# Per-block tile counts, GpSimd's share and the planner's activity thresholds, changed together in a fused linear-attention and softmax-attention kernel

## Chip, core and metric

The kernel runs on one core of one Trainium2 chip. The metric is the device time of one execution in microseconds. Several executions are made, and their median is the time of the kernel.

## What is computed

There are two attention layers over the same input x (2048 rows, 512 columns, 32 heads of 16), mixed row by row by a gate:

```python
g = sigmoid((x * gate_w).sum(-1, keepdims=True))
# A: linear attention with softmax feature maps
phi_q = concat([softmax(q_A @ w_phi), softmax(-q_A @ w_phi)])   # phi_k alike
o_A = phi_q @ (phi_k.T @ v_A) / (phi_q @ phi_k.sum(0) + 1e-6)
# B: softmax attention, per head
p = softmax(q_B @ k_B.T * 16 ** -0.5)
o_B = p @ v_B
out = g * (o_A @ wo_A) + (1 - g) * (o_B @ wo_B)
```

Layer B needs 32 x 2048 x 2048 exponentials, and these set the work of ScalarE.

## The kernel before

**Tiling of B.** The heads come in four rows of eight. A block is one chunk of 512 queries with four heads, so that there are 32 blocks (NB). A block has 64 tiles: four heads times sixteen groups of 128 keys, each a 128 x 512 piece of the transposed scores. A score matmul (line 782) contracts only 16 of 32 rows, so up to four heads run beside each other in row strips of the array. The product with v (pv_mm, line 895) writes 32 rows of the one PSUM bank psO for each head, and four heads run beside each other in column strips. psO collects the whole block. When the block is complete, VectorE copies psO to Tf (line 979, add_norm), and only then can the next block start in psO.

**Two ways to an exponential.** Most tiles go to ScalarE. They are dealt in slots of alternately three and two tiles (line 727). A slot is one score op qk (add_qk), one ACTIVATE over the 3 or 2 PSUM banks (add_exp, line 874) and, for up to three slots together, one pv op (add_pv). The remaining tiles go to VectorE. DN, line 30, says how many of each block. They are taken in groups of four, the last of a block possibly of two (line 708). In a group, each tile has its own first step from PSUM to 16-bit integers (D1, line 840), and the group shares a mask (D2, line 855), a second mask (D3, line 857) and a product (D4). The product runs on VectorE (line 860), or, for the first PN[b] full groups of a block, as four quarters on GpSimd (line 863). Each VectorE tile gives two matmuls into psO (add_pvd, "term" ops); the block's last pv op waits for all of them.

**Buffers of the groups.** A group takes one buffer of each of three rings (line 747). Before block 13 (G_EARLY) the first two rings hold four buffers each, later four and three. make_groups(n) opens groups up to number n, and stops at the first whose buffers are still held. When a block opens in psO, groups are asked for up to the block's last number plus G_DEEP (line 968).

**Beside it.** Projections of B, the whole of layer A (phi, kv_half, q_rest), and the output projection (out_tile, out_part, out_last) are given to the same planner as fill ops, with due times counted in slots.

**The planner.** Plan.layout simulates the five engines with given durations and writes down an order for each engine; emit turns the orders into instruction streams with semaphore waits. On PE it chooses by priority: qk first, then what else is ready, and nothing that would make the next qk late (QK_TOL). It keeps a figure for the activity of PE over the last 3.41 us of its own time (WINDOW), as a weighted share:

```python
active = sum(w * (y - max(x, t - WINDOW)) for x, y, w in streams) / WINDOW
```

ACTIVE holds four thresholds for it. If PE has nothing to do and active is below ACTIVE[0], a round of four matmuls on the zero tile (line 885) is put in, into psO while a block is open there, otherwise into a free miscellaneous bank. Ahead of a pv op of an open block, more such rounds can stand:

```python
if op.room and t > 20.0 and active < ACTIVE[1]:
    op.extra = min(op.room, 1 if active > ACTIVE[2] else 2)
```

Riding means that an op shares a pass of the array with the one before it, in strips that this leaves free. The planner then counts only 0.02 us for it. Terms have exactly the priority T_PRIO, so that for them the last condition decides:

```python
if o.kind == want and not used_heads & set(o.heads) and o.ready <= pe_start + RIDE_TOL and (
        o.kind == "dq" or o.prio < T_PRIO or active >= ACTIVE[3]):
```

A first step's priority is its block's first slot minus D_AHEAD = 22 slots (d_prio), so VectorE works about one block ahead of ScalarE.

Of the kernel before, what the change touches and what calls it, by code (L numbers as in the profile page):

```python
# [26 lines left out]
EXPB = 127.0 * 2.0 ** 7 - 75.0  # L27
ESCALE = math.log(2.0) / 2.0 ** 7

DN = (0, 10, 14, 16, 14, 16, 14, 16, 14, 16, 14, 16, 14, 16, 14, 16, 14, 16, 14, 16, 14, 16, 14, 16, 14, 16, 14, 16, 14, 16, 14, 12)  # L30
G_EARLY = 13
W_AT = 18.0
D_FIRST = 12
# [1 line left out]
WINDOW = 3.41  # L35
ROWS = (0.0, 0.42, 0.65, 1.0, 1.15)
COLS = (0.0, 0.9, 1.25, 1.55, 1.55)
ACTIVE = (1.0, 0.64, 0.62, 0.54)
PE_CLASS = {"qk": 0, "dq": 0, "pv": 1, "term": 1, "zero": 1}
T_PRIO = 40.0  # L40
WARM = 4
# [8 lines left out]
DMA_PAD, T2_PAD = 1.0, 1.5  # L50
QK_TOL = (0.2, 0.65)
TURN_PAD = 4.0
G_DEEP = 6
K_AT, K_PACE, Q_AT, Q_PACE = 45.0, 13.0, 275.0, 13.5
PN = (1, 2, 1, 2, 1, 2, 1, 2, 1, 2, 1, 2, 1, 2, 1, 2, 1, 2, 1, 2, 1, 2, 1, 2, 1, 2, 1, 2, 1, 2, 1, 2)
D_AHEAD = 22.0
CONT = -60.0
EPAIRS = 5
# [44 lines left out]
class Plan:  # L103
# [44 lines left out]
    def layout(self):  # L148
# [19 lines left out]
        while left:  # L168
# [30 lines left out]
            for e in ENGINES:  # L199
# [11 lines left out]
                if e == "pe" and last_pe is not None and busy[e] > t - 1e-6:  # L211
                    want = {"qk": "dq", "dq": "dq"}.get(last_pe, "term")
                    for item in sorted(queues[e]):
                        o = item[2]
                        if o.kind == want and not used_heads & set(o.heads) and o.ready <= pe_start + RIDE_TOL and (
                                o.kind == "dq" or o.prio < T_PRIO or active >= ACTIVE[3]):
                            if o.acq is not None:
# [36 lines left out]
                busy_qk = e == "pe" and t < qk_at and t + 0.32 > qk_at + QK_TOL[qk_slot]  # L254
                if pick is None and e == "pe" and not busy_qk and zero_ok and t > 20.0 and active < ACTIVE[0]:
                    pick = Op("pe", 0.215, 1e9, self.idle, "idle")
# [4 lines left out]
                    left += 1  # L261
                if pick is None and e == "pe" and not busy_qk and not zero_ok and t > 20.0 and active < ACTIVE[0]:
                    bs = [b for b in self.misc if b.free and b.shared and all(o.end + LAT <= t for o in b.last)]
# [23 lines left out]
                if e == "pe":  # L287
                    if op.room and t > 20.0 and active < ACTIVE[1]:
                        op.extra = min(op.room, 1 if active > ACTIVE[2] else 2)
                        op.full += 0.215 * op.extra  # L290
# [110 lines left out]
def _build(ctx, nc, A_x, A_wqkv, A_w_phi, A_wo, B_wqkv, B_wo, gate_w, out):  # L401
# [295 lines left out]
    slots = []  # L697
    assert all(n % 2 == 0 for n in DN)
    dcount = [[0] * 4 for _ in range(NB)]
    dtiles, groups, turn = [], [], 0  # L700
    for b in range(NB):
        for k in range(DN[b]):
            i = (k + turn) % 4
            dcount[b][i] += 1
            dtiles.append(dict(t=(b, i, NT - dcount[b][i]), k=k))
        turn += DN[b]
        mine = dtiles[len(dtiles) - DN[b]:]
        for n in range(0, DN[b], 4):
            groups.append(dict(ts=mine[n:n + 4], left=len(mine[n:n + 4]), pool=n // 4 < PN[b] and len(mine[n:n + 4]) == 4))
    cur, rot = 0, 0  # L710
# [104 lines left out]
    def make_groups(n):  # L815
        for g in groups[made[0]:n]:
            if any(k in holder and holder[k]["left"] for k in (g["t"], g["s"])):
                break
            holder[g["t"]] = holder[g["s"]] = g
            add_group(g)  # L820
            made[0] += 1

    def d_prio(d):
        b = d["t"][0]
        return first_slot[b] + d["k"] * 20.0 / DN[b] - D_AHEAD

# [88 lines left out]
    def add_pv(js):  # L915
# [4 lines left out]
        for b, jmts in parts.items():  # L920
# [38 lines left out]
            if b not in full_start and all((b, i) in pv_started for i in range(4)):  # L959
# [7 lines left out]
                if mine:  # L967
                    make_groups(mine[-1]["g"]["n"] + G_DEEP)
            if js[0] == 0:
# [388 lines left out]
```

## Time and profile before

| what | us |
|---|---|
| median of 5 runs | 782.19 |
| lowest, highest | 780.57, 783.93 |
| the profiled execution | 781.67 |
| its span, first to last instruction | 779.8 |
| ACT busy | 758.3 |
| PE busy | 753.6 |
| DVE busy | 676.0 |
| POOL busy | 352.2 |
| mean granted TensorE clock, share of full | 0.991 |

The span is shorter than the profiled execution's time, because the time also holds what lies around the instructions. Busy times are of one engine each and overlap. ACT is ScalarE, PE is TensorE (PEld its weight loads), DVE is VectorE and POOL is GpSimd. A busy PE includes the zero matmuls. The profile also gives the clock that TensorE was granted in each stretch, as a share of full speed.

### The profile page before, as it was taken

Reading aid. Unit: us, or ns where it says so; the run is one execution under the profiler, and the core shown is the slowest. Engines: PE = TensorE matmul, PEld = TensorE weight load, DVE = VectorE, ACT = ScalarE, POOL = GpSimd, SP = SyncE. Lnnn points to the kernel's source line nnn. Section 1 sums busy time; section 2 is a strip of 40 time slices with the busy share of each in tenths; the row PEclk is TensorE's granted clock in tenths of the full one; section 3 lists DMA queues with packets and bytes.
Section 4 is the critical chain, followed back from the end, with each engine's and each line's share of the span. In section 5 each row is a group of like instructions: output and inputs, shape, how many; then the busy total and the mean of one; then the engine's idle time right before and its main releaser. Section 6 shows DMA issues by size and latency. Waiting matters only on the chain.

```text
span 779.8 us, 17665 instructions
## 1 busy us (share of the span) xinstructions
PE 753.6 (97%) x7342; PEld 232.5 (30%) x7342; DVE 676.0 (87%) x1098; ACT 758.3 (97%) x708; POOL 352.2 (45%) x329
## 2 busy tenths in 40 slices
PE   8999999999999999999999999999999999999999
PEld 4332223323332222333222232223223223222223
DVE  3678898899989999799999897999999899899793
ACT  5999999999999999999999998999999999999995
POOL 6133634536354564443734626455364443124332
PEclk9999999999999999999999998999999999999999
DMA  6600001000000000200001312231322231020001
GB/s 128 145 9 16 20 11 24 9 19 12 9 17 10 23 8 9 71 8 23 23 24 47 74 54 45 61 58 60 71 69 61 52 77 36 29 57 16 24 21 48
DMA packets 67935, 30.74 MB, mean 39 GB/s; under 512 B 53208, under 2 KB 62808, under 8 KB 67856
## 3 DMA queue, kind: packets, MB, share of 16 engines
q1 hardware_dynamic: 66368, 28.95, 15.6%
q8 instruction: 57, 0.93, 0.5%
q10 hardware_dynamic: 1104, 0.66, 0.3%
q14 instruction: 22, 0.18, 0.1%
q0 software_dynamic: 384, 0.02, 0.1%
HBM read 7.87 MB, written 8.88 MB: 21 GB/s over the span
## 4 chain that ended last, share of the span: by engine, by line
ACT 76%; PE 19%; DVE 3%; issue 1%; DMA 0%; SPq 0%; DVEq 0%
ACT E_t L874 72%; PE psS L782 6%; PE psO L895 6%; ACT EA_t L1117 4%; PE psO L885 3%; PE psS L590 2%; PE psM L590 2%; DVE Tx_t L840 1%; PE psM L782 1%; DMA phiK_t<-in_A_x_dram 0%; DVE oA_t L1205 0%; PE psS L1231 0%; DVE Ty_t L857 0%; DVE vA_t L855 0%; PE psM L885 0%
## 5 line engine op out<-in xcount | busy, mean ns | idle before, releaser
L874 ACT ACTIVATE E_t<-psS 128x1536 bf16<-128x1536 f32 x637 | 729.7, 1340 | 6.8 <-PE psS L782 5.3
L782 PE MATMUL psS<-qz_t,kTB_t 32*128 32x512 bf16 x1816 | 286.7, 386 | 19.3 <-ACT E_t L874 15.8
L863 POOL TENSOR_TENSOR Tx_t<-Tx_t,vA_t 128x512 bf16<-128x512 bf16 x116 | 132.9, 1167 | 125.2 <-DVE Ty_t L857 48.4
L885 PE MATMUL psO<-xT_t,zero_t 128*32 128x512 bf16 x1720 | 150.8, 385 | 0.0
L782 PEld LDWEIGHTS psS<-qz_t,kTB_t 32*128 32x128 bf16 x1816 | 71.5, 91 | 250.3 <-ACT E_t L874 196.6
L895 PE MATMUL psO<-E_t,vaug_t 128*32 128x512 bf16 (+1 forms) x1592 | 140.8, 389 | 0.2 <-DVE vaug_t L646 0.2
L840 DVE TENSOR_SCALAR Tx_t<-psM 128x512 int16<-128x512 f32 x129 | 87.7, 679 | 12.2 <-PE psM L782 9.3
L840 DVE TENSOR_SCALAR Tx_t<-psS 128x512 int16<-128x512 f32 x119 | 81.2, 682 | 11.0 <-PE psS L782 9.3
L782 PE MATMUL psM<-qz_t,kTB_t 32*128 32x512 bf16 x232 | 89.5, 386 | 1.0 <-DVE qz_t L687 0.5
L863 POOL TENSOR_TENSOR oT_t<-oT_t,WoB_t 128x512 bf16<-128x512 bf16 x44 | 51.2, 1181 | 51.8 <-DVE oT_t L857 27.5
L1122 POOL TENSOR_TENSOR half_t<-EA_t 128x512 f32<-128x512 bf16 x32 | 37.0, 1156 | 61.3 <-ACT EA_t L1117 32.1
L885 PEld LDWEIGHTS psO<-xT_t,zero_t 128*32 128x32 bf16 x1720 | 38.6, 94 | 63.9 <-issue 53.4
L1130 POOL TENSOR_TENSOR phiK_t<-EA_t,stat_t 128x512 bf16<-128x512 bf16 x32 | 34.9, 1090 | 44.3 <-DVE WoB_t L855 13.5
L895 PE MATMUL psO<-Tx_t,vaug_t 128*32 128x512 bf16 x248 | 53.2, 394 | 0.0
L995 POOL TENSOR_TENSOR oT_t<-Tf_t,Rb_t 128x512 bf16<-128x512 f32 x15 | 19.1, 1272 | 68.9 <-DVE vA_t L860 48.0
L895 PEld LDWEIGHTS psO<-E_t,vaug_t 128*32 128x32 bf16 (+1 forms) x1592 | 29.3, 95 | 58.1 <-issue 53.0
L863 POOL TENSOR_TENSOR Tx_t<-Tx_t,WoB_t 128x512 bf16<-128x512 bf16 x28 | 31.8, 1155 | 31.7 <-DVE Ty_t L857 20.8
L1130 POOL TENSOR_TENSOR phiQ_t<-EA_t,stat_t 128x512 bf16<-128x512 bf16 x32 | 33.9, 1058 | 26.5 <-DVE stat_t L1126 8.6
L857 DVE TENSOR_SCALAR Ty_t<-Tx_t 128x2048 int16<-128x2048 int16 x50 | 39.3, 796 | 0.1
L895 PE MATMUL psO<-Ty_t,vaug_t 128*32 128x512 bf16 (+1 forms) x284 | 38.8, 386 | 0.0
L782 PEld LDWEIGHTS psM<-qz_t,kTB_t 32*128 32x128 bf16 x232 | 21.1, 91 | 33.8 <-issue 12.9
L840 DVE TENSOR_SCALAR WAT_t<-psM 128x512 int16<-128x512 f32 x39 | 26.7, 684 | 4.8 <-PE psM L782 4.3
(184 smaller groups left out, 910.1 us busy)
## 6 DMA issues: line engine op xcount, KB each, us to landing
dpq<-phiQ_t SPq DMA_DIRECT2D x16, 256.0 KB, 2.2
Rb_t<-lr SPq DMA_DIRECT2D x120, 32.0 KB, 1.8
dpo<-oA_t SPq DMA_DIRECT2D x16, 128.0 KB, 1.8
qz_t<-qz_t SPq DMA_DIRECT2D x120, 16.0 KB, 1.8
Tf_t<-Tf_t SPq DMA_DIRECT2D x60, 32.0 KB, 2.0
out_dram<-WvA_t SPq DMA_DIRECT2D x14, 128.0 KB, 1.7
WB_t<-in_B_wqkv_dram SPq DMA_DIRECT2D x3, 384.0 KB, 4.9
WvA_t<-in_A_wqkv_dram SPq DMA_DIRECT2D x1, 512.0 KB, 4.0
```

Of the source, the lines that this page charges most:

```text
L590: return [lambda e, ap, i=i: e.matmul(ap, lhsT=lhs[i], rhs=rhs[i], start=(i == 0), stop=(i == len(lhs) - 1)) for i in range(len(lhs))]
L782: return e.matmul(bank, lhsT=kT_B[32 * i:32 * i + 32, b // 8 % 2, 128 * kt:128 * (kt + 1)], rhs=qz[32 * i:32 * i + 32, b // 2 % 4, b % 2, ...
L840: ops.append(drain(f, mm, "dve", 0.70, d_prio(d), lambda e, ap, q=q: e.tensor_scalar(quarter(tb, q).bitcast(I16), ap, EXPB, 0.0, op0=ALU.a ...
L857: add(0.72 if full else 0.45, lambda e: e.tensor_single_scalar(shaped(si16, si16), shaped(ti16, si16), 0x7F80, ALU.bitwise_and), tk, [g["s ...
L863: ops.append(P.add("pool", 1.1, d_prio(g["ts"][0]) - 5.0, lambda e, q=q: e.tensor_tensor(quarter(t4, q), quarter(t4, q), quarter(m4, q), A ...
L874: op = P.add("act", 0.051 + 0.4267 * n, 0.0, lambda e: e.activation(Ebuf[:, j // 2 % EPAIRS, 1536 * (j % 2):1536 * (j % 2) + 512 * n], psS ...
L885: ins = e.matmul((psO if bank is None else bank)[32 * i:32 * i + 32, :], lhsT=zero[:], rhs=xT[:, 0, 0:NQ], start=bank is not None, stop=ba ...
L895: return e.matmul(psO[32 * i:32 * i + w, :], lhsT=vaug[:, kt, o:o + w], rhs=rhs, start=start, stop=stop, tile_position=(0, 32 * i), skip_g ...
L995: P.add("pool", 1.1, -40, lambda e: e.tensor_tensor(oT[:, r, qc, :], Tf[:, 0, :], Rb[:], ALU.mult), reads=[("Tf", 0), "Rb"], writes=[("oT" ...
L1117: ins = e.activation(EA[:, b, :].rearrange("p (g s c) -> p s g c", s=2, c=64)[:, sgn, :, :], ap.rearrange("p (g c) -> p g c", c=64), ACTF. ...
L1122: P.add("pool", 1.15, prio, lambda e: e.tensor_tensor(half[:], e3[:, :, 0:8], e3[:, :, 8:16], ALU.add), reads=[("EA", b)], writes=["half"] ...
L1130: parts.append(P.add("pool", 1.0, prio, lambda e, n=n: e.tensor_tensor(dst[:, 512 * n:512 * n + 512].rearrange("p (g f) -> p g f", f=DH), ...
```

## The change

Only five constants of the planner are changed. DN sets how many tiles of each of the 32 blocks are taken by VectorE. PN sets how many of a block's full groups have their product on GpSimd. ACTIVE holds the thresholds described above. G_DEEP says how many groups beyond a block are asked for ahead.

```diff
-DN = (0, 10, 14, 16, 14, 16, 14, 16, 14, 16, 14, 16, 14, 16, 14, 16, 14, 16, 14, 16, 14, 16, 14, 16, 14, 16, 14, 16, 14, 16, 14, 12)
+DN = (0, 10, 12, 16, 10, 16, 12, 16, 14, 16, 14, 16, 14, 16, 14, 16, 14, 16, 14, 18, 14, 16, 14, 16, 14, 18, 12, 18, 14, 16, 18, 14)
...
-ACTIVE = (1.0, 0.64, 0.62, 0.54)
+ACTIVE = (1.0, 0.66, 0.72, 0.2)
...
-G_DEEP = 6
+G_DEEP = 5
...
-PN = (1, 2, 1, 2, 1, 2, 1, 2, 1, 2, 1, 2, 1, 2, 1, 2, 1, 2, 1, 2, 1, 2, 1, 2, 1, 2, 1, 2, 1, 2, 1, 2)
+PN = (2, 2, 1, 2, 1, 2, 1, 2, 1, 2, 1, 2, 1, 2, 1, 2, 1, 2, 1, 2, 0, 2, 1, 2, 1, 2, 1, 2, 2, 2, 1, 0)
```

In DN the entries of blocks 2, 4, 6, 19, 25, 26, 27, 30 and 31 differ; in PN those of blocks 0, 20, 28 and 31. No instruction is written differently; the planner lays out all streams anew from these values.

## Prediction

> **What bounds the kernel now.** I read first the page's busy times, then ScalarE's waits, then ScalarE and the clock by stages, then the chain that ended last, then the groups by form. The page's first part:
>
> ```profile
> span 779.8 us, 17665 instructions
> PE 753.6 (97%) x7342; PEld 232.5 (30%) x7342; DVE 676.0 (87%) x1098; ACT 758.3 (97%) x708; POOL 352.2 (45%) x329
> ```
>
> ACT and PE both show 97%, but PE's share contains filler: the group of matmuls on the zero tile (line 885) alone is 150.8 us busy. The waits of ScalarE:
>
> ```profile
> ACT E_t L874 <- PE psS L782: 5.3, 5, 2.0
> ACT WvA_t L1065 <- PE psS L590: 5.1, 1, 5.1
> ACT xT_t L1220 <- PE psS L1214: 2.5, 2, 1.3
> ...
> ACT qz_t L669 <- PE psM L662: 2.0, 1, 2.0
> ACT E_t L874 <- PE psM L782: 0.8, 1, 0.8
> ACT E_t L874 <- PE psO L895: 0.2, 1, 0.2
> ```
>
> Columns: total us, times, longest. Of the 5.3 us, 2.0 stand ahead of the very first exp (timeline: it starts at 11.73 us). All that ScalarE loses to PE between the first and the last exp is therefore 5.3 - 2.0 + 0.8 + 0.2 = 4.3 us. Where? The stages of 20 us (busy us and counts of PE, PEld, DVE, ACT, POOL; then the granted TensorE clock) are full for ACT except here:
>
> ```profile
> 440.00:460.00 20.00, 19.12 (x190) 5.55 (x189) 17.26 (x37) 19.47 (x18) 11.24 (x11) 0.91 0.20 52
> 460.00:480.00 20.00, 18.98 (x170) 5.18 (x169) 16.44 (x36) 17.65 (x17) 8.99 (x8) 0.83 0.14 43
> ...
> 720.00:740.00 20.00, 19.08 (x170) 5.29 (x169) 14.45 (x23) 18.87 (x18) 8.04 (x8) 0.91 0.09 23
> ```
>
> ACT lacks 0.53, 2.35 and 1.13 us, 4.0 of the 4.3, in just the three stages whose clock is below 1. Cut finer, the second is
>
> ```profile
> 469.51:472.92 3.41, 3.04 (x10) 0.67 (x10) 2.14 (x5) 3.31 (x4) 3.41 (x4) 0.66 0.03 5
> 472.92:476.33 3.41, 3.41 (x23) 0.59 (x22) 1.76 (x3) 1.95 (x2) 1.35 (x2) 0.50 0.05 12
> ```
>
> The clock is at half, and ACT works 1.95 of 3.41 us. The mean clock of 0.991 gives (1 - 0.991) x 779.8 / 0.5 = 14 us at half clock in all, about four stretches of 3.4 us. Each of the three places follows the copy of psO to Tf (line 979) that ends a block: 444.85, 468.99 and 727.83 us in the timeline. The copies run from 42.2 (block 0) to 727.8 (block 29), 23.6 us apart, so these are the ends of blocks 17, 18 and 29. While psO is being copied and has no open block, the planner has no bank for its zero matmuls, and PE stood empty for about 0.7 us at 445.4 and 468.9, 0.6 at 728.3.
>
> The remaining span is head (11.73 us), ScalarE's own work, and a tail of 779.8 - 770.7 = 9.1 us from the last exp's end.
>
> **What the Trainium skill says.** "TensorE: Matmul & The Clock Gate", Part 1, says that an activity monitor gives the array half its pulses after an idle window and that the window is 3.41 us and free-running. The trace agrees on the size: the clock is 0.50 over such a stretch and is full again after one or two. It also means that where a dip falls in the window matters, so the count of half-clock stretches can differ between executions; the five times (780.57 to 783.93) spread by about the price of two or three. "ScalarE: Activation LUTs", the section on what ACT_TABLE_LOAD costs, gives 0.833 ns an element[...]; the forms below differ by 1550 - 1131 = 419 ns for one tile more. "Advanced Engine Details and Errata", VectorE Performance Modes, says that GpSimd and VectorE's two-port forms block each other on a shared port; the trace shows line 857 at a mean of 796 ns in the Ty group and 0.68 where undisturbed.
>
> ```profile
> L874 ACT ACTIVATE E_t<-psS 128x1536 bf16<-128x1536 f32 x318 | 492.8, 1550 | 6.7 <-PE psS L782 5.3 <-PE psM L782 0.8 <-PE psO L895 0.2
> L874 ACT ACTIVATE E_t<-psS 128x1024 bf16<-128x1024 f32 x319 | 360.7, 1131 | 0.1
> ```
>
> **The change part by part.** *DN, the tile counts.* The sum goes from 456 to 458 of 2048 tiles, so ScalarE has 1590 instead of 1592. They are dealt in slots of 3 and 2: 318 x 5 = 1590, so exactly one two-tile exp goes (637 to 636). The page has 729.7 us for 637, 1.146 mean; a two-tile slot is half a tile below the mean, 1.146 - 0.5 x 0.419 = 0.94 us. It lies on the path: **-0.9 us**. VectorE gets 2 more first steps (0.68 each), and counting groups of four gives 106 full ones as before and 17 halves instead of 16, one half more at 0.44 + 0.42 + 0.73: +3.0 us in all. Blocks 2, 4 and 6 have 8 tiles fewer, blocks 19, 25, 27, 30 and 31 12 more, 26 two fewer. The early relief buys nothing by itself: at 100 to 120 us DVE is at 19.80 of 20 while ACT has 20.00.
>
> *PN, whose product runs on GpSimd.* Counting min(PN, full groups): 47 groups on GpSimd become 45. Block 28 gains one, 20 loses one, 31 loses two; 30 keeps one, and PN[0] meets no group. GpSimd loses 8 quarters x 1.17 = 9.3 us, VectorE gains 2 x 1.3 = 2.6. Together DVE goes to about 676 + 5.6 = 681.6 us, still 87% of the span. A product takes 4.49 us as four quarters on GpSimd (timeline at 467.7), 1.3 on VectorE: about 3 us sooner for the terms of blocks 20 and 31. Cover: ACT does not wait on GpSimd in any row.
>
> *The last two blocks*, where cover is thinnest. Blocks 30 and 31, before: 26 first steps x 0.68, 6 full groups x 1.57 (lines 855 and 857 together), one half at 0.86, 3 full products x 1.3 and a half at 0.73 = 32.6 us of DVE. After: 32 x 0.68 + 7 x 1.57 + 2 x 0.86 + 6 x 1.3 + 2 x 0.73 = 43.8. So +11.2 us. The stages from 700 to 760 have 60 - (19.03 + 14.45 + 19.81) = 6.7 us of DVE idle, and 760 to 771 about 8.3 more (6.25 busy in that stage, some 3.5 of it after 772): 15 us of room for 11.2. I take it as hidden, at 0; its bounds are 0 and +5 (rival 2). Nothing below 0, since the tail from the last exp does not shorten: the last terms already ran at 765.9, 6 us before the last pv matmul at 771.97.
>
> *ACTIVE[1] 0.64 to 0.66, ACTIVE[2] 0.62 to 0.72.* A pv matmul in a planned lull gets zero rounds ahead of it: now always two, and in lulls up to 0.66. Each round is 0.22 us of PE (the spacing of such rounds in the timeline). Behind a pv on PE stands the next qk, and ScalarE waits for that. PE itself waits for ScalarE 196.6 us in 470 waits (line 782's loads), 0.42 us each, so one round fits in one such wait and two nearly do; only lulls between 0.62 and 0.66 change. Bounds: -1 us (a drop avoided) and +1 (five qk late by 0.2); I take 0 by itself.
>
> *ACTIVE[3] 0.54 to 0.2.* The second-kind products (terms, lines 895) may now share a pass with a pv matmul of other columns even in a lull. At the third drop this can be seen in the chain:
>
> ```profile
> 730.35 2.25 PE psO L895 x15
> 732.60 0.55 PE psS L782 x4
> ```
>
> 2.25 us of pv and term matmuls at half clock stand ahead of the qk for which ScalarE then waits 1.13 us. At half clock a pass takes 0.43 (spacing at 730.7 to 731.5), so two or three terms that ride instead of running alone give 0.8 to 1.3 us back there. PE gets empty earlier elsewhere, but while a block is open that is filled by zero matmuls.
>
> *G_DEEP 6 to 5.* Nothing: groups may be opened only while their buffers are free, and the rings hold four before block 13 and three afterwards (Ty, Ty, vA). Five ahead was never reached.
>
> *What is moved.* All five streams are laid out anew, and every block end from block 2 on moves by some us against the free-running window. The edits fall on the places of the drops: first steps run 22 slots (25 us) ahead, so block 19's two tiles and block 20's product lie at 445 to 490, those of blocks 28 to 31 at 680 to 760.
>
> **Sum.** The profiled execution took 781.67 us (span 779.8 and 1.9 around it), 0.52 below the median of 782.19. Likeliest: one exp less, -0.9, and three of the four half-clock stretches gone, at 4.3 / 4 = 1.1 each, -3.3: 781.67 - 4.2 = 777.5, put on the median's level 778.0. With none left it is -0.9 - 4.3: 777.0 on that level; head and tail stay.
>
> **Rivals.** (1) *The dips stay.* 28 of 31 block ends pass without a drop and three do not; a new layout may draw three again, elsewhere, and the riding term removes activity just in a lull. For it: at the three places no zero rounds precede the last pv matmuls (at 442.9, 467.9, 727.2), so the planner counted more activity than its 0.64 there, and 0.66 need not catch it. Then only the exp goes: 782.19 - 0.9 = 781.3. (2) *VectorE ends last*, the slower side. If the room at 723 to 733 us can't be used (there DVE waits for PE and GpSimd), the last two blocks' 11.2 us meet the 6 to 8 us behind 761 us, and the last pv waits; from 6 us of lateness each further one is one on the end. Up to 11.2 - 6 = 5.2 us, less 0.9 for the exp: 786.5; it beats the noise bound from 9.3 us of lateness. Against it: the products leave a slow GpSimd chain, and GpSimd no longer blocks VectorE there. (3) *Only part of the drops goes*, two stretches of four: -0.9 - 2.2, 779.1.
>
> **Chances.** Likeliest case, with three or all stretches gone, 0.44; rival 3 0.17; rival 1 0.23; rival 2, with which I count more drops than before, 0.16. A measurement of this kernel can tell about 0.3%, 2.35 us, from no change: faster means below 779.8. Rival 3 sits near that bound, and I give it two thirds above it in gain: faster 0.55, same 0.29, slower 0.16. The range runs from 775.6 (no half clock, rides and zero rounds giving 1 us more) to 783.8 (as many drops, and some of rival 2).
>
> **What would show it.** Right: 636 exps, mean clock near 0.998, ScalarE's waits on line 782 between first and last exp near 1 us, DVE near 681.6, GpSimd's line 863 at 180 quarters (now 188), the last exp's end near 766.5, the tail still 9 us. Wrong: a mean clock of 0.991 or lower (rival 1); a tail above 10 us with the last term after the last exp (rival 2); ScalarE waits for qk where the clock is full, which would mean that the zero rounds delay it.

## Result and the profile after

The kernel after has a median of 777.35 us, the one before 782.25 over the executions made beside it: ratio 0.9949, 95% interval 0.9937 to 0.9961. Forecast were 778.0 and a range of 775.6 to 783.8. Run once more beside other kernels it gave 777.56 against 782.59, ratio 0.9943 (0.9919 to 0.9967). One execution of each kernel took about 3 ms (3284.58 and 2864.64 us) and is left out of every count below.

The profiled execution, however, took 779.47 us, above the median, and its record does not show what was forecast: its clock is 0.991, as before. The page's first part and ScalarE's waits:

```profile
span 777.7 us, 18039 instructions
PE 756.1 (97%) x7528; PEld 232.1 (30%) x7528; DVE 672.6 (86%) x1105; ACT 757.1 (97%) x707; POOL 342.5 (44%) x321
```

```profile
ACT E_t L874 <- PE psS L782: 6.5, 6, 1.7
ACT WvA_t L1065 <- PE psM L590: 4.0, 1, 4.0
```

The next two views are the exps by form and a piece of the chain that ended last. The piece has score matmuls in the part of the span where, before, such matmuls stood behind 2.25 us of psO matmuls:

```profile
L874 ACT ACTIVATE E_t<-psS 128x1536 bf16<-128x1536 f32 x318 | 493.6, 1552 | 7.1 <-PE psS L782 6.5
L874 ACT ACTIVATE E_t<-psS 128x1024 bf16<-128x1024 f32 x318 | 360.6, 1134 | 0.1
```

```profile
741.37 0.76 PE psO L895 x11
742.13 0.59 PE psS L782 x4
```

One two-tile exp is gone, as counted. The place in the chain lies within block 30, not at its start (block 29 was copied from psO at 726.5 us). At full clock 0.76 us of psO matmuls are ahead of the score matmuls, and no such pile stands in the chain between 697.9 us and here: there ScalarE runs 38 exps on end. These are the stages of 20 us that are furthest from full for ACT between head and tail:

```profile
320.00:340.00 20.00, 17.94 (x196) 6.81 (x192) 11.75 (x20) 18.75 (x18) 9.20 (x8) 0.91 0.09 19
...
580.00:600.00 20.00, 19.33 (x186) 5.55 (x178) 16.96 (x38) 17.28 (x16) 8.73 (x8) 0.78 0.17 55
600.00:620.00 20.00, 19.87 (x205) 5.64 (x202) 17.21 (x32) 19.11 (x18) 8.18 (x8) 0.96 0.23 49
```

All three places of before (440, 460, 720) are full now, but there are new ones at 330 and at 593 to 602. The second one, cut finer:

```profile
588.82:592.23 3.41, 2.91 (x28) 0.87 (x27) 3.38 (x9) 3.41 (x4) 2.05 (x2) 0.85 0.12 27
592.23:595.64 3.41, 3.41 (x28) 0.90 (x25) 3.10 (x8) 2.63 (x3) 1.06 (x1) 0.50 0.30 90
595.64:599.05 3.41, 3.41 (x26) 0.80 (x27) 2.11 (x4) 2.47 (x2) 0.00 (x0) 0.50 0.25 84
```

Read the order in time. PE has a hole of 0.5 us (2.91 of 3.41) while ACT is still full; the clock falls; only then does ACT miss 0.8 and 0.9 us. Again the copy of psO to Tf, at 588.37, stands just ahead. So the mechanism of the prediction is there, and this execution drew four stretches by chance.

The other profiles show the same order. Twelve of the fourteen have one to four times at half clock, of one to four stretches each and 30 in all (of the experiments below, e4 has none and e11 has 26 alone). Take for each the window of 3.413 us that ends where the clock falls. TensorE is busy for 2.0 to 2.75 us of it, where the median window of these profiles has 3.3 or 3.4. ScalarE is busy for the whole of it in 29 of the 30 cases. So the clock falls while ScalarE still has work, and ScalarE's waits come afterwards. Idleness of this size does not always bring a half clock: in the profile of before the window that ends at 661.71 us has only 2.50 us of PE, and the clock stays full behind it.

A second profiled execution of the kernel after has one stretch:

```profile
span 775.6 us, 17985 instructions
PE 744.4 (96%) x7474; PEld 232.8 (30%) x7528; DVE 672.2 (87%) x1105; ACT 756.7 (98%) x707; POOL 342.1 (44%) x321
```

```profile
ACT WvA_t L1065 <- PE psM L590: 4.0, 1, 4.0
ACT E_t L874 <- PE psS L782: 3.1, 3, 1.9
```

Of its 3.1 us, 1.9 are ahead of the first exp. Apart from the head, the two profiles of after differ in the time at half clock and in what ScalarE waits, and in little else. The table splits each profiled span into the time to the first exp (head), ScalarE's busy and idle time from there to the end of the last exp, and the rest (tail):

| profile | stretches at half clock | head | ACT busy | ACT idle | tail | span |
|---|---|---|---|---|---|---|
| before | 4 | 11.73 | 754.12 | 4.83 | 9.12 | 779.8 |
| after, first | 4 | 9.99 | 752.78 | 5.54 | 9.39 | 777.7 |
| after, second | 1 | 12.05 | 752.35 | 1.82 | 9.38 | 775.6 |
| e4 below | 0 | 10.08 | 752.10 | 0.64 | 10.68 | 773.5 |

**Counting stretches in every execution.** Each execution reports its span and mean clock. (1 - clock) x span / (0.5 x 3.41) is the number of half-clock stretches, to about half a one. The 27 executions of the kernel after divide like this: 13 with one (median 777.1 us), 7 with two (777.2), 3 with three (778.6), 2 with four (780.2), one each with five (782.4) and seven (784.1). The mean is 2.1, and the straight line through them is 775.3 us plus 1.24 for each stretch. The kernel before, over 68 executions beside the first four experiments, has 14 with three (780.9), 11 with four (781.3), 32 with five (783.6), 11 with more; the mean is 4.6. None of these had fewer than three.

### The profile page after: what moved, and what is told of

The parts are those of the page before. It is cut to its first block, busy times and chain, and to the rows that moved or that the text cites. A ratio compares the mean times of both kernels' runs of the same rounds, so it can differ in the third digit from the quotient of the medians.

```text
span 777.7 us, 18039 instructions
## 1 busy us (share of the span) xinstructions
PE 756.1 (97%) x7528; PEld 232.1 (30%) x7528; DVE 672.6 (86%) x1105; ACT 757.1 (97%) x707; POOL 342.5 (44%) x321
## 4 chain that ended last, share of the span: by engine, by line
ACT 59%; PE 35%; DVE 3%; issue 1%; POOL 1%; DMA 1%; SPq 0%; POOLq 0%
ACT E_t L874 56%; PE psS L782 11%; PE psO L895 9%; PE psO L885 6%; ACT EA_t L1117 3%; PE psM L590 3%; PE psS L590 3%; PE psM L782 2%; DVE Tx_t L840 1%; DMA phiK_t<-in_A_x_dram 1%; POOL WAT_t L863 0%; DVE vA_t L840 0%; DVE vA_t L860 0%; DVE vA_t L855 0%; DVE WAT_t L840 0%
## 5 line engine op out<-in xcount | busy, mean ns | idle before, releaser
L885 PE MATMUL psO<-xT_t,zero_t 128*32 128x512 bf16 x1824 | 157.5, 387 | 0.0
L863 POOL TENSOR_TENSOR Tx_t<-Tx_t,vA_t 128x512 bf16<-128x512 bf16 x68 | 79.2, 1192 | 55.2 <-DVE Ty_t L857 23.1
L840 DVE TENSOR_SCALAR Tx_t<-psS 128x512 int16<-128x512 f32 x123 | 83.9, 682 | 14.1 <-PE psS L782 12.3
L863 POOL TENSOR_TENSOR Tx_t<-Tx_t,WoB_t 128x512 bf16<-128x512 bf16 x52 | 58.7, 1157 | 75.0 <-DVE Ty_t L857 65.7
L782 PE MATMUL psM<-qz_t,kTB_t 32*128 32x512 bf16 x224 | 86.1, 385 | 1.3 <-DVE WAT_t L840 0.8
L840 DVE TENSOR_SCALAR Tx_t<-psM 128x512 int16<-128x512 f32 x109 | 74.4, 682 | 12.4 <-PE psM L782 6.5
L863 POOL TENSOR_TENSOR WAT_t<-WAT_t,vA_t 128x512 bf16<-128x512 bf16 x32 | 37.2, 1187 | 43.6 <-DVE Ty_t L857 23.7
L895 PE MATMUL psO<-Tx_t,vaug_t 128*32 128x512 bf16 (+1 forms) x232 | 38.5, 385 | 0.0
L857 DVE TENSOR_SCALAR Ty_t<-Tx_t 128x2048 int16<-128x2048 int16 (+1 forms) x49 | 33.6, 685 | 0.0
L840 DVE TENSOR_SCALAR WAT_t<-psS 128x512 int16<-128x512 f32 x40 | 27.3, 681 | 2.7 <-PE psS L782 2.0
```

Source lines behind the costliest of these rows:

```text
L782: return e.matmul(bank, lhsT=kT_B[32 * i:32 * i + 32, b // 8 % 2, 128 * kt:128 * (kt + 1)], rhs=qz[32 * i:32 * i + 32, b // 2 % 4, b % 2, ...
L840: ops.append(drain(f, mm, "dve", 0.70, d_prio(d), lambda e, ap, q=q: e.tensor_scalar(quarter(tb, q).bitcast(I16), ap, EXPB, 0.0, op0=ALU.a ...
L857: add(0.72 if full else 0.45, lambda e: e.tensor_single_scalar(shaped(si16, si16), shaped(ti16, si16), 0x7F80, ALU.bitwise_and), tk, [g["s ...
L863: ops.append(P.add("pool", 1.1, d_prio(g["ts"][0]) - 5.0, lambda e, q=q: e.tensor_tensor(quarter(t4, q), quarter(t4, q), quarter(m4, q), A ...
L885: ins = e.matmul((psO if bank is None else bank)[32 * i:32 * i + 32, :], lhsT=zero[:], rhs=xT[:, 0, 0:NQ], start=bank is not None, stop=ba ...
L895: return e.matmul(psO[32 * i:32 * i + w, :], lhsT=vaug[:, kt, o:o + w], rhs=rhs, start=start, stop=stop, tile_position=(0, 32 * i), skip_g ...
```

## Experiments

The change touches four constants, DN, PN, ACTIVE and G_DEEP (not five, as the section on the change says). The planner's orders answer part of the question without a run. With G_DEEP back at 6, or PN[0] back at 1, the kernel after has the same order on every engine; so it has with ACTIVE[1] and ACTIVE[2] back at 0.64 and 0.62, and the kernel before with 0.66 and 0.72 is itself. Only DN, PN at blocks 20, 28 and 31, and ACTIVE[3] do anything.

In the results, "n stretches" is the mean number over all executions of that kernel, and "line" is the straight line through its executions, time against number of stretches.

**e1, DN alone.**

```diff
-DN = (0, 10, 14, 16, 14, ..., 16, 14, 12)
+DN = (the new one)
```

> The kernel before with only the new DN (458 tiles on VectorE, 636 exps). My theory (one exp less, and the rest of the gain is fewer half-clock stretches): 781.3 if the clock record stays like that of before (four stretches, mean 0.991), 778 if it goes to one stretch (0.998). Rival (VectorE's relief in blocks 2 to 6 and its shorter waits give the gain at full clock): about 777.5 with a clock still near 0.991.

781.96 us, ratio 0.9984 (0.9968 to 1.0001), 3.8 stretches. As in the first case of my theory: one exp less, the clock nearly as bad, and little gained. By count: two stretches 777.9, four 781.3, five 783.2, so that at four and five it is within 0.4 us of before (781.3, 783.6). VectorE's relief gives nothing that shows at an equal number of stretches, and the rival is wrong.

**e2, PN alone.**

```diff
-PN = (1, 2, 1, 2, ..., 1, 2)
+PN = (the new one)
```

> The kernel before with only the new PN (two products fewer on GpSimd, one each moved at blocks 20 and 28). Mine: within 1.5 us of before, 780.8 to 783.8, since ScalarE never waits for GpSimd; any difference must show in the number of half-clock stretches. Rival (the shorter product chain in block 31 ends the kernel earlier): 779, with a tail behind the last exp 3 us shorter than 9 us.

782.88, ratio 0.9993 (0.9976 to 1.0011), and 6.5 stretches. Three of the 22 executions are much longer than the others (787.25 to 789.95, ten and eleven stretches); without them it is 781.71 and 5.8, anything from one (775.5) to nine (785.9). The time hardly moves because the new order draws more stretches, while its line starts lower: 775.1 plus 1.19 each without those three. The tail of its profile was 8.2 us, 0.9 shorter than before and not 3.

**e3, ACTIVE[3] alone.**

```diff
-ACTIVE = (1.0, 0.64, 0.62, 0.54)
+ACTIVE = (1.0, 0.64, 0.62, 0.2)
```

> The kernel before with only ACTIVE[3] at 0.2, so that terms may share a pass in a planned lull. Mine: 1 to 2 us faster than before, 780.3 to 781.3, by a lower price of each half-clock stretch. Rival (riding takes activity away just in a lull): more half-clock stretches, mean clock below 0.991, 783 to 785.

778.71, ratio 0.9957 (0.9936 to 0.9978), 3.1 stretches. More than I expected, and for another reason: a stretch costs 1.34 us here as well (before: 1.13 to 1.38 in its three sets), so that riding does not make stretches cheaper. There are fewer, and the line starts at 774.8. The rival is wrong too: riding did not take the clock away. Why there are fewer is not shown.

**e4, the kernel after without the ride.**

```diff
-ACTIVE = (1.0, 0.66, 0.72, 0.2)
+ACTIVE = (1.0, 0.64, 0.62, 0.54)
```

> The kernel after with the old ACTIVE[3] = 0.54 (new DN and PN, no riding in lulls). Mine: 778 to 779, the ride being worth about 1 us. Rival (the ride is what keeps the clock): 781.3, as before less one exp. Rival (the ride costs activity): 776, faster than the kernel after.

778.36, ratio 0.9949 (0.9932 to 0.9966), 1.8 stretches. The new DN and PN together give nearly all that the whole change gives; the ride adds nothing that can be told from noise, though alone it was worth 0.4%. The edits do not add up. This kernel's profile had no stretch at all, and the waits of its ScalarE are the cleanest evidence for what bounds the kernel:

```profile
ACT WvA_t L1065 <- PE psS L590: 4.4, 1, 4.4
ACT L1220 <- issue: 2.3, 1, 2.3
ACT xT_t L1220 <- PE psS L1214: 2.3, 2, 1.2
ACT E_t L874 <- PE psS L782: 1.7, 1, 1.7
ACT qz_t L669 <- PE psM L662: 0.9, 1, 0.9
```

The one wait of an exp, 1.7 us, is the first exp's. At full clock no other exp waits for PE by this view.

**e5, more activity at block ends.** The order of all engines is that of before.

```diff
-for m, t in enumerate(ts):
+for m, t in list(enumerate(ts)) * (2 if j in ends else 1):
...
-for _ in range(zero_ops[j, b].extra):
+for _ in range(2 if last and old else zero_ops[j, b].extra):
```

> The kernel before, same order on all engines, only more matmuls at block ends: two zero rounds ahead of a block's last pv op, and the score matmuls of the four slots behind each block's first slot issued twice into the same banks. Mine (half-clock stretches at block ends set the time): stretches fall from 4.6 on average to below 2, and the time to 777 to 779 although PE does more. Rival (work that comes late sets the time, and the half clock only goes with it): PE is later by 0.2 to 0.4 us at every block end, 783 to 787.

802.15, ratio 1.025 (1.0219 to 1.028), with one stretch in each of six executions. The clock was held as I expected, and the time rose by 20 us, four times what I had given the rival. In its profile ScalarE is idle for 19.95 us between first and last exp at a clock of 0.998, where e8's, also with one stretch, has 1.82. The waits stand at the block ends. 31 ends x 4 doubled score ops is 124, so they come to 18 / 124 = 0.15 us for each (the zero rounds ahead of the last pv ops may have a part in it; they were not tried alone). ScalarE's busy time is 6.0 us longer as well, and I have not tested why. As a test of the clock it was badly built, since the activity was put on the very instruction that ScalarE waits for. What it shows is that score ops at block ends have little slack.

**e6, weaker filler.** Order as before.

```diff
 def zero_mm(e, bank=None):
-    for i in range(4):
+    for i in range(1):
```

> The kernel before, same order on all engines, only the filler weaker: a zero round between other work issues one matmul instead of four. Nothing that anything waits for is added. Mine: at least twice as many half-clock stretches, 10 or more, and 1.2 to 1.6 us for each one more, 789 or above. Rival: with less work on PE the time stays at 782 or falls.

782.28, ratio 0.9991 (0.997 to 1.0012), 6.0 stretches. I was wrong in size: a quarter of the filler brings only 1.4 stretches more, and not twice as many. The rival has the time right, but not because less work is free of cost: the line starts at 773.7, against 776.1 for before in the same set, and the added stretches take this back. So four strips of filler cost about 2 us at equal clock, and hold the clock little better than one.

**e7, shorter exps.** Eight slots leave out 960 of their 1024 columns.

```diff
-... 1536 * (j % 2) + 512 * n], psS[:, 512 * base:512 * (base + n)], ACTF.Exp
+... 1536 * (j % 2) + w], psS[:, 512 * base:512 * base + w], ACTF.Exp   # w = 64 in eight slots
```

> The kernel before with eight two-tile exps, spread between slots 85 and 585, cut from 1024 to 64 columns; their other columns are left out. Mine (ScalarE's own work is the path, and one exp of 0.94 us is worth 0.94): 8 x 0.79 = 6.3 us less at an equal number of half-clock stretches, about 776. Rival (PE's and VectorE's queues are as full, and ScalarE's time comes back as waits): less than 3 us, above 779.

780.59, ratio 0.9972 (0.9956 to 0.9988), 4.3 stretches. Of the 6.3 us some 2 were gained. This is the rival's number. The stages of this kernel show where the rest is. They are at full clock, hold one short exp each (slots 85 and 145), and were full for ACT before, or nearly (20.00 and 19.93):

```profile
100.00:120.00 20.00, 18.58 (x178) 5.33 (x177) 19.80 (x29) 19.42 (x19) 6.08 (x6) 1.00 0.06 14
...
180.00:200.00 20.00, 18.95 (x186) 5.69 (x176) 18.77 (x29) 19.24 (x21) 13.26 (x12) 1.00 0.04 9
```

Idle of 0.58 and 0.76 us: ScalarE then waits for the scores of the next slots. A shortened exp is worth little. PE has only two sets of score banks to run ahead in, which I take for the reason; it was not tested. It does not price a slot that goes with its score op, as the change's does, so it does not settle the exp term.

**e8, the kernel after again.**

> The kernel after once more, beside the others on one chip. Mine: 777 to 778, two half-clock stretches on average, and each run's time on a line of about 775.5 us plus 1.2 to 1.6 us for each stretch. Rival: the first set of runs was a lucky one, 779 or above with three or more stretches.

777.56, 1.9 stretches, line 775.2 plus 1.37 each. As expected.

**e9 and e10, which entries of PN, on top of the new DN.**

```diff
-PN = (..., 1, 2, 1, 2, ...)   # the old one
+PN[20] = 0                    # e9
+PN[28], PN[31] = 2, 0         # e10
```

> The kernel before with the new DN and of PN only block 20 (its product on VectorE). DN alone had 3.8 half-clock stretches on average and 782.0, DN and the whole PN 1.8 and 778.4. Mine (each edit shifts the order behind it, and the gain is the number of stretches that the new order happens to have): the stretch near 473 us of the DN kernel, at block 19, goes, the later ones may stay, 2 to 3 on average, 779 to 781. Rival (block 31's product on VectorE gives the gain): as DN alone, 782 with near 4.

> The kernel before with the new DN and of PN only blocks 28 and 31. Mine: the stretch near 473 us stays and one or two of those at 661 and 709 go, 2 to 3.5 on average, 779 to 781.5. Rival (block 31's product on VectorE gives the gain): 778.4 with 1.8 stretches, as with the whole PN.

e9: 780.84, ratio 0.9984 (0.997 to 0.9998), 3.0 stretches. e10: 781.28, ratio 0.9981 (0.9966 to 0.9995), 2.8. DN alone had 3.8, both together (e4) 1.8. Each half takes away about one stretch, and block 31's product is not what makes the gain. The places were as I had said in e10's profile (473 and 660 stayed, 709 was gone), but not in e9's: the one at 473 us was still there, and that at 593 lasted 10 us.

**e11, no filler.** Order as before.

```diff
-for i in range(4): e.matmul(psO[32 * i:32 * i + 32, :], lhsT=zero[:], rhs=xT[:, 0, 0:NQ], ...)
+for i in range(1): e.matmul(psO[32 * i:32 * i + 32, 0:1], lhsT=zero[:], rhs=xT[:, 0, 0:1], ...)
```

> The kernel before, same order on all engines, each zero round cut from four matmuls of 512 columns to one of a single column, so that PE has almost no filler. Mine (PE's idleness lowers the clock, and the clock makes ScalarE wait): 15 half-clock stretches or more and 1.2 to 1.6 us for each, 793 or above, with ScalarE's waits on line 782 in those stretches. Rival (ScalarE's wait comes first, the half clock only follows it): filler is taken away and nothing is added, so 779 to 782.

838.86, ratio 1.0713 (1.0673 to 1.0752). Four of the six executions have 79 stretches at a mean clock of 0.838 and a median of 838.0; the other two have 100 and took 858. Work was only taken away, and nothing waits for what that work computes, yet the kernel lost 56 us. In the profile ScalarE's idle time between first and last exp rose from 4.8 to 53.0 us, its busy time from 754.1 to 763.4. ScalarE's waits:

```profile
ACT E_t L874 <- PE psS L782: 46.0, 65, 1.9
ACT E_t L874 <- PE psM L782: 5.4, 7, 1.4
```

and two of its stages, where before has ACT at 20.00 and the clock at 1.00:

```profile
60.00:80.00 20.00, 19.84 (x141) 5.80 (x141) 15.42 (x25) 17.89 (x18) 4.82 (x5) 0.76 0.06 15
80.00:100.00 20.00, 19.02 (x113) 4.89 (x111) 16.18 (x26) 18.47 (x18) 10.63 (x10) 0.74 0.05 15
```

With the order in time that the section on the result shows, this gives the direction: idleness of PE, then the clock, then ScalarE's waits. When the stretches are that many, each costs (838.0 - 776) / 79 = 0.8 us, an estimate in which 776 is about where the line of before starts (776.1 in the set of e5 to e8).

**e12, the kernel after with weaker filler** (the edit of e6).

> The kernel after with zero rounds of one matmul instead of four. In the kernel before this gave 1.4 stretches more, but 2.4 us less at an equal number (773.7 against 776.1 when drawn down to none). Mine: both again, 776 to 777.5, no slower than the kernel after. Rival (the four strips are needed to hold the clock): four stretches or more, above 779.

778.45, ratio 0.9942 (0.992 to 0.9963), 2.1 stretches in nine executions. That is not told apart from the kernel after, and above the 776 to 777.5 that I expected.

## Why the prediction was right, and where it was not

**The time and the main term.** The forecast sum was one exp (-0.9) and three stretches of four at 1.1 each (-3.3). Measured: the mean goes from 4.6 to 2.1 or 1.9 stretches, so about 2.6 fewer, at 1.13 to 1.38 us in these two kernels; 2.6 x 1.3 = 3.4. Count and price were each a little off and their product right. That the clock is the cause follows from e11, from the order of events in twelve profiles, and from e4: without half clock ScalarE's exps wait for PE only at the start.

**The exp term.** It was forecast at 0.94 us, and the runs do not measure it well. ScalarE's busy time between first and last exp is 753.7 to 754.2 us in the profiles of before, e2, e3 and e6 (637 exps) and 751.9 to 753.3 in those of after, e1, e4, e8, e9, e10 and e12 (636). The means differ by 1.4, single profiles by 0.4 to 2.3.

In the times the term can't be seen alone. To compare kernels at an equal number of stretches, I put lines of one common slope through those that ran beside each other (1.23 to 1.32 us a stretch in the three sets). Of the kernels with one exp less, after (e8) then lies 1.0 us below before, e1 0.5 and e4 0.1 below, but e9 0.5 and e10 1.0 above. With no exp less, e2 and e3 lie 2.1 and 1.6 below (standard errors 0.2 to 0.4). So at an equal clock a new layout moves the time by more than one exp is worth. One part of that is the tail: 8.2 us in e2 and e3, 9.1 in before, 10.6 to 11.1 in e1, e4 and e9. For the kernel after, the stretches (3.4) and all the rest (1.0) make 4.4; the medians differ by 4.9.

**VectorE.** Forecast 681.6 us, measured 672.6. Counting was right (458 first steps, 312.5 us; products 61 x 1.34), but I priced the mask steps (lines 855 and 857) at the old mean. In the full groups they fell from 85.2 + 83.3 to 79.0 + 77.9 us. The term that was mis-sized is "the new tiles at the old rows' durations". DN alone gives the same fall (81.2 + 76.6) with GpSimd unchanged at 351 us, so less work on GpSimd isn't the reason; which instructions run beside them may be, and that I have not tested. GpSimd itself is at 342.5 as worked out (352.2 - 9.3).

**The last two blocks.** Taken at 0, bounds 0 and +5: tail 9.12 before, 9.39 and 9.38 after. Rival 2 did not happen. But of the four kernels with the new DN and no ride, e1, e4 and e9 had 10.6 to 11.1 and only e10 had 9.6. So the cover was thin: without the ride the last blocks' tail was mostly 1.5 to 2 us longer.

**The thresholds.** Here my reasons failed. I said of ACTIVE[1] and ACTIVE[2] that zero rounds in lulls up to 0.66 change; no instruction changes. I said of ACTIVE[3] that riding terms cheapen a stretch; e3 shows the same price and fewer stretches, and e4 against the kernel after shows no gain from it in the new order. The 0 for G_DEEP was right for the reason given.

**Rival 1** is what e1 and e2 did: the layout was redrawn and the dips stayed. I had argued that the edits fall on the places of the drops. All three places did go, but new ones came (330, 593), and PN alone drew more stretches than before. A stretch at 332 to 334 us stands in both profiles of after and in those of e1, e9 and e10, and in none with the old DN: it comes with the new one. That the sum of the edits would draw few was a chance rightly weighed, not something that I had derived.

**Still open:** which instructions at a block end decide whether a dip is deep enough, and why PE runs empty there (that the planner had no bank for its zero matmuls was read from the code and not tested). Each of DN, PN and the ride moves the count, singly by -0.9, +1.2 (e2 without its three longest executions) and -1.5, together by -2.6; I have no rule that gives these numbers.

## What to carry to other kernels

When the bounding engine waits only in stages where TensorE's clock is below 1, count half-clock stretches per execution and price a change by how many it leaves and by what it takes off the bounding engine; do that over many executions, because one profile draws the count at random. Filler matmuls are worth their place as far as they hold the clock: without them this kernel lost 56 us (e11), but three quarters of them bought 1.4 stretches and cost about as much (e6). Matmuls put on or ahead of an instruction that the bounding engine waits for can cost far more than the clock they save (e5). Before explaining an edit to a planner's constants, compare the orders it produces: four of the edited values here changed nothing.

## What the runs showed of the hardware

One program (e2) had between one and nine half-clock stretches, for 775.5 to 786.9 us, even with its three longest executions left out. "TensorE: Matmul & The Clock Gate" (the Trainium skill, Part 1) says that the window is free-running, and the traces agree. In each of the twelve profiles all half-clock times begin a whole multiple of 3.413 us apart, to within 0.001 us, and this grid lies elsewhere in every execution. Each of the 30 begins between 0.4 us before and 3.3 us after the start of a copy of psO to Tf.

Block 12's copy, near 331 us, shows the draw. All seven profiles with the new DN have it between 330.1 and 332.1 us. In five a line of the grid falls 1.7 to 2.2 us after its start, and there the clock drops. In e4 and e12 the line falls 0.8 and 2.7 us after it, and it does not. (e4's grid is read from a half-clock record behind its last instruction.)

One zero matmul in one 32-column strip held the clock almost as well as four side by side (6.0 against 4.6 stretches), while one of a single column did not (79 and more).

The head has a slow time of its own. The first exp began at 9.7 to 10.2 us in seven of the fourteen profiles and at 11.7 to 12.2 in the other seven. The reason is in PE's timeline of the head (start, duration, count). Of before:

```profile
8.14 1.06 PE L662 MATMUL psM<-xT_t,WB_t 128*128 128x256 bf16 x4
9.00 0.99 PE L662 MATMUL psO<-xT_t,WB_t 128*128 128x256 bf16 x4
```

The same two groups of after, in its first profile:

```profile
7.22 0.60 PE L662 MATMUL psM<-xT_t,WB_t 128*128 128x256 bf16 x4
7.65 0.60 PE L662 MATMUL psO<-xT_t,WB_t 128*128 128x256 bf16 x4
```

Before's first projections still ran at about half speed, after's no longer did. The first group took 1.04 to 1.06 us in the seven profiles that began late and 0.60 in the seven others. These 1.7 us between the two profiles belong to neither kernel: e8, the same kernel as after, began at 12.05. The clock column reads 1.00 for the first 20 us of both, so that in the head the speed must be read from the matmuls.
